# Sketched attention and a ReLU expert layer: token order taken at the PSUM reads, and other edits

## The chip, the cores and the metric

The kernel runs on one core of a Trainium2 chip. The metric is device time in microseconds. Engines are named as the profile names them: PE is TensorE (matmuls; its weight loads are PEld), DVE is VectorE, ACT is ScalarE, POOL is GpSimd, SP issues most of the transfers. Every engine works through its instructions in the order in which the program gives them.

## What is computed

For each of 4 batches and 4 heads (1088 tokens, 32 features) keys and queries go through two small matrices S1 and S2 (8 x 32), and the feature of a token is the product of all pairs. Attention without softmax follows, and then a layer on all 4352 tokens:

```python
def phi(x):
    a = np.einsum('rd,bhsd->bhsr', S1, x)
    b = np.einsum('rd,bhsd->bhsr', S2, x)
    return np.einsum('bhsi,bhsj->bhsij', a, b).reshape(*x.shape[:-1], r * r)
q_p, k_p = (phi(q), phi(k))
kv = np.einsum('bhsf,bhsd->bhfd', k_p, v)
z = np.sum(k_p, axis=2)
num = np.einsum('bhsf,bhfd->bhsd', q_p, kv)
den = np.einsum('bhsf,bhf->bhs', q_p, z)[..., None] + 1e-06
x = num / den                       # (4352, 128) after heads are put side by side
h = x @ w_in                        # 128 -> 2048
g = np.maximum(h, 0.0) + alpha * np.minimum(h, 0.0)
return g @ w_out                    # 2048 -> 128
```

## The kernel before

Every piece of work is an `op` with an engine (or several), a planned duration, what it depends on, and the buffers it uses. `plan` places the ops one after the other by those planned numbers and thereby fixes the order of instructions on each engine and the buffer that each gets; the chip then runs that fixed order. An op that may run on ACT or DVE goes to the one where the plan has it end sooner.

PSUM has eight banks. Bank 7 collects the output of the expert layer. The other seven are shared: `ph` gives banks to the expert layer's first matmuls (four at most), `pa` all banks of the attention (six at most).

**Keys** (`keys`, `kfeat`), per batch and pair of heads: DVE turns the keys block by block (`turn`, L482, tile kT); PE forms both small features (L450); an evacuation puts them in tile ab (L216 on ACT or L218 on DVE); POOL, or DVE for the first half of batch 0, multiplies all pairs (L463, tile kp); PE then forms kv (L500, L508, with L514 and L517 for the last 64 tokens). Small steps on DVE, ACT and PE (zm L528 to L531, fin L537 and L538, zz L547 and L548) make the weights kvW and zc.

**Queries** (`queries`, `q_main`), per batch: DVE turns all 1024 columns (L557, tile qT). PE forms the first feature, round *a*, in eight array tiles of 32 x 64 with 512 columns each (L564, `rnd`). Two ACT copies bring round a to SBUF (L216, tile aq, 128 x 1024 each). Round *b* forms the second feature, in two ops of four tiles each. Two DVE multiplications (L577) read b from PSUM and multiply it into aq. Then PE forms den and num (L592), DVE turns the denominators (L601, called dT), takes reciprocals (L607, L608), spreads them (L610) and multiplies (L615, tile xT, bf16). Batch 0 does the part from den on in two halves. The moving operand of rounds a and b is read in the order h, t, j, so neighbouring columns are 32 elements apart in qT.

**Expert layer** (`mlp`), 8 chunks of 512 tokens and one of 256: 16 times a matmul with w_in (L675), a relu on ACT (L681) or DVE (L683) into tile rh, and a matmul with w_a (L693), then one with W (L689); DVE turns the result (L699) and SP stores it. As alpha * min(h, 0) = alpha * h - alpha * max(h, 0), w_a is w_out times (1 - alpha), and W is w_in times alpha * w_out; both are computed at the start from the loaded weights (L385 and L394, POOL and ACT; L410, L421).

**Start.** SP issues the loads in the order of the program: k0 in two halves, v0 in four pieces of 256-byte rows, the rests, w_in, w_out, then k, q and v of batches 1 to 3. ACT issues the small rows and q0. Until the expert layer begins, matmuls on a zero tile (L332, warming matmuls) fill PE's order, their number set by the plan's gaps.

Of the kernel before, what the change touches and what calls it, by code (L numbers as in the profile page):

```python
# [48 lines left out]
OWN = 80  # L49
AHEAD = {"pe": 120, "act": 150, "dve": 250, "pool": 300, "sp": 0}  # L50


def plan(ops, classes):
# [39 lines left out]
    while waiting:  # L93
        shut, can = set(), []
        for o in waiting:
# [8 lines left out]
            fits = []  # L104
            for e in o.eng:
                t = max([at, free_at[e]] + [d.end + SEM if d.on != e else d.free if e == "pe" else d.end + OWN for d in o.deps])
                fits.append((t + o.dur[e], t, e))
            end, t, e = min(fits)
# [31 lines left out]
def kernel(  # L140
# [40 lines left out]
    def pa(n=1):  # L181

        return Buf("ps", n, "pa", PA_MOST, [6, 0, 1, 2, 3, 4, 5] if n == 1 else [0, 2, 4])
# [10 lines left out]
    def sb(b):  # L194
        return tiles[b.cls][b.slot]

    PA_MOST, PH_MOST = 6, 4
# [31 lines left out]
    state = {"t": 2800.0}  # L229
    loads = {}  # L230

    def load(name, eng, dst, src, nbytes, rate=290.0):
        if nbytes < 1 << 14:
            t = 3500.0
# [42 lines left out]
    def load_v(b):  # L277
        for t in range(4):
# [10 lines left out]
    load_main("q", q_sb, q, 0, "act")  # L289
    load_v(0)  # L290
    load_rest("k", k_rs[0], k, 0)
    load_rest("v", v_rs[0], v, 0)
    load("w_in", "sp", w_in_f, moe_w_in, 1 << 20)
    load("w_out", "sp", w_out_f, bass.AP(tensor=moe_w_out.tensor, offset=moe_w_out.offset,
                                         ap=[[DM, 128], [DM * 128, NC], [1, DM]]), 1 << 20)
    for b in range(1, B):
        load_k(b)
# [177 lines left out]
    def keys(b, due, kp_eng):  # L475
        halves = []
        for hp in range(2):
# [44 lines left out]
        bs, bz, bf = Buf("fs"), Buf("fs"), pa()  # L522
# [260 lines left out]
```

## Time and profile before

| | |
|---|---|
| median of 3 runs | 142.74 us (140.89 to 142.9) |
| the profiled execution | 143.26 us, of which the span of the trace is 141.3 us |
| busy in the span | PE 92%, DVE 65%, ACT 52%, POOL 16% |
| mean granted clock of PE | 0.953 of full |
| first and last matmul of the expert layer | 23.9 us and 133.9 us |

Times in the rows below are microseconds from the start of the span, or durations. [...] A matmul of f32 data shows as two instructions, since it takes two passes. In the chain that ended last each row lasts until the next link begins, so successive matmuls show their true spacing there, while the groups give the duration of single instructions, which overlap.

### The profile page before, as it was taken

What the parts mean: (1) busy time and instruction counts of PE and PEld (TensorE: products, weight loads), DVE (VectorE), ACT (ScalarE), POOL (GpSimd) and SP (SyncE); (2) the same over time, 40 slices, a digit from 0 to 9 for tenths busy, and PEclk for the clock granted to TensorE, in tenths of its full rate; (3) what the DMA queues carried; (4) which work ended last, traced back from release to release, by engine and by line L of the source; (5) the groups of instructions that cost most, each with busy time, mean ns of one, the idle gap of its engine ahead of it and who ended that gap; (6) DMA issues with size and microseconds to landing.
All of it is one profiled execution on the core that took longest, in us unless ns stands there. A gap on an engine that the chain in (4) does not pass through costs nothing.

```text
span 141.3 us, 3073 instructions
## 1 busy us (share of the span) xinstructions
PE 130.2 (92%) x1222; PEld 55.9 (40%) x1237; DVE 92.3 (65%) x168; ACT 72.8 (52%) x139; POOL 22.4 (16%) x20
## 2 busy tenths in 40 slices
PE   6999998999998999999999999999999999999910
PEld 2376142667212337543143364440423444445500
DVE  3661469999996797585468954174658957777500
ACT  3020466992644577637136676280437686666610
POOL 2005068790000000900000009000000000000000
PEclk9999999999999999999959999997579999999995
DMA  3989993899600400400004004000040040130400
GB/s 120 285 148 369 312 274 57 248 262 321 102 14 0 77 0 0 74 5 0 5 0 74 0 1 73 5 0 0 5 74 0 0 74 0 27 56 2 75 12 25
DMA packets 33906, 11.22 MB, mean 79 GB/s; under 512 B 28884, under 2 KB 33252, under 8 KB 33764
## 3 DMA queue, kind: packets, MB, share of 16 engines
q1 hardware_dynamic: 33252, 10.49, 31.6%
q10 hardware_dynamic: 640, 0.54, 1.2%
q8 instruction: 9, 0.15, 0.5%
q14 instruction: 5, 0.04, 0.1%
HBM read 8.80 MB, written 2.23 MB: 78 GB/s over the span
## 4 chain that ended last, share of the span: by engine, by line
PE 88%; DVE 2%; POOL 2%; issue 2%; ACT 2%; ACTq 0%; DVEq 0%
PE ps L675 23%; PE ps L693 23%; PE ps L564 15%; PE ps L592 7%; PE ps L332 6%; PE ps L450 5%; PE ps L500 3%; PE ps L689 2%; POOL kp__71 L463 2%; PE ps L421 1%; PE ps L514 1%; PE ps L410 1%; PE ps L538 1%; DVE dt__78 L601 1%; DVE rr__80 L610 1%
## 5 line engine op out<-in xcount | busy, mean ns | idle before, releaser
L681 ACT ACTIVATE rh__82<-ps 128x512 bf16<-128x512 f32 (+1 forms) x36 | 21.3, 592 | 16.5 <-PE ps L675 14.2
L675 PE MATMUL ps<-xT__94,w_in_bf 128*128 128x512 bf16 (+1 forms) x77 | 27.0, 369 | 1.9 <-DVE xT__94 L615 0.6
L675 PEld LDWEIGHTS <-w_in_bf 128*128 128x128 bf16 x144 | 14.3, 101 | 26.1 <-issue 15.6
L693 PEld LDWEIGHTS <-w_a_bf 128*128 128x128 bf16 x144 | 14.2, 102 | 26.2 <-issue 14.2
L675 PE MATMUL ps<-xT__95,w_in_bf 128*128 128x512 bf16 x62 | 23.3, 383 | 0.5 <-issue 0.4
L681 ACT ACTIVATE rh__83<-ps 128x512 bf16<-128x512 f32 (+1 forms) x26 | 14.7, 564 | 12.4 <-PE ps L675 11.2
L564 PE MATMUL ps<-qT__74,Sab 32*64 32x512 f32 x96 | 17.8, 1044 | 0.0
L693 PE MATMUL ps<-rh__82,w_a_bf 128*128 128x512 bf16 (+1 forms) x44 | 16.7, 380 | 0.1
L683 DVE TENSOR_SCALAR rh__84<-ps 128x512 bf16<-128x512 f32 (+1 forms) x17 | 10.6, 625 | 7.6 <-PE ps L675 7.3
L681 ACT ACTIVATE rh__84<-ps 128x512 bf16<-128x512 f32 x22 | 13.1, 596 | 4.3 <-PE ps L675 4.2
L683 DVE TENSOR_SCALAR rh__83<-ps 128x512 bf16<-128x512 f32 x16 | 11.0, 691 | 6.2 <-PE ps L675 6.2
L693 PE MATMUL ps<-rh__83,w_a_bf 128*128 128x512 bf16 (+1 forms) x38 | 14.2, 374 | 0.1
L463 POOL TENSOR_TENSOR kp__70<-ab__67 128x1024 f32<-128x1024 f32 x3 | 5.9, 1954 | 49.6 <-ACT ab__67 L216 49.6
L693 PE MATMUL ps<-rh__84,w_a_bf 128*128 128x512 bf16 (+1 forms) x36 | 13.7, 380 | 0.0
L216 ACT COPY aq__76<-ps 128x1024 f32<-128x1024 f32 (+1 forms) x8 | 6.7, 850 | 11.1 <-PE ps L564 11.1
L332 PE MATMUL ps<-zero 128*128 128x512 bf16 x38 | 11.1, 439 | 1.3 <-DVE tab L324 1.2
L577 DVE TENSOR_TENSOR aq__76<-ps,aq__76 128x1024 f32<-128x1024 f32 (+1 forms) x8 | 8.2, 1022 | 5.3 <-PE ps L564 5.3
L463 POOL TENSOR_TENSOR kp__71<-ab__68 128x1024 f32<-128x1024 f32 x4 | 8.1, 2033 | 8.9 <-ACT ab__68 L216 8.7
L681 ACT ACTIVATE rh__85<-ps 128x512 bf16<-128x512 f32 (+1 forms) x11 | 5.7, 521 | 2.9 <-PE ps L675 2.8
L683 DVE TENSOR_SCALAR rh__82<-ps 128x512 bf16<-128x512 f32 (+1 forms) x10 | 6.1, 612 | 1.7 <-PE ps L675 1.5
L699 DVE STREAM_TRANSPOSE oT__91<-ps 128x512 f32<-128x512 f32 x8 | 5.7, 716 | 2.2 <-PE ps L689 1.8
L332 PEld LDWEIGHTS <-zero 128*128 128x128 bf16 x39 | 4.0, 112 | 7.3 <-issue 3.6
(113 smaller groups left out, 169.5 us busy)
## 6 DMA issues: line engine op xcount, KB each, us to landing
out_dram<-oT__91 SPq DMA_DIRECT2D x34, 64.0 KB, 1.9
v<-in_v_dram SPq DMA_DIRECT2D x16, 128.0 KB, 5.5
k<-in_k_dram SPq DMA_DIRECT2D x3, 512.0 KB
q<-in_q_dram SPq DMA_DIRECT2D x3, 512.0 KB, 7.0
w_in_f<-in_moe_w_in_dram SPq DMA_DIRECT2D x1, 1024.0 KB, 5.0
k<-in_k_dram SPq DMA_DIRECT2D x2, 256.0 KB, 2.9
q<-in_q_dram ACTq DMA_DIRECT2D x1, 512.0 KB, 6.0
kr<-in_k_dram SPq DMA_DIRECT2D x4, 32.0 KB, 3.4
```

The costliest lines, as they stand in the source:

```text
L216: nc.scalar.copy(dst, src)
L332: nc.tensor.matmul(PS[:, 7], zero[:, :128], zero, start=True, stop=True, skip_group_check=True)
L450: nc.tensor.matmul(ps(bf)[:, j * 64:(j + 1) * 64], sb(bT)[:, j * 128:(j + 1) * 128], S12blk.rearrange("p h c -> p (h c)"), start=True, sto ...
L463: (nc.vector if e == "dve" else nc.gpsimd).tensor_tensor(out=dst, in0=i0, in1=i1, op=ALU.mult)
L564: nc.tensor.matmul(dst, bview(Sab[32 * t:32 * t + 32, i], [[1, R]]), moving(sb(bq), t, c), start=True, stop=True)
L577: mu.append(op("dve", dv(2 * nf), lambda e, x=x: nc.vector.tensor_mul(sb(aq)[:, 2 * x:2 * x + 2, :nf], ps(b2[x])[:, :, :nf], sb(aq)[:, 2 * ...
L592: nc.tensor.matmul(dst, w, mv, start=True, stop=True, skip_group_check=True)
L675: nc.tensor.matmul(ps(b)[:, :n], w_in_bf[:, c * 128:(c + 1) * 128], xs(), start=True, stop=True)
L681: nc.scalar.activation(sb(br)[:, :n], ps(b)[:, :n], ACTF.Relu)
L683: nc.vector.tensor_scalar_max(sb(br)[:, :n], ps(b)[:, :n], 0.0)
L693: nc.tensor.matmul(ps(bo)[:, :n], w_a_bf[:, c], sb(hs[c][1])[:, :n], start=c == 0, stop=False)
L699: o = op("dve", dv(n), lambda e: nc.vector.transpose(bview(sb(boT), [[1, n]]), ps(bo)[:, :n]), [last], [bo, boT], 80, t0 + TG * n / 512, f ...
```

## The change

- `moving` for the main queries reads qT in the order h, j, t: runs of 16 neighbouring elements. The columns of a and b therefore stand in PSUM in the order h, j, t, and the two ACT copies (`told`, `line`) and the two DVE multiplications read PSUM with a step of 16 elements and write aq in the order that den and num read as before.
- Round b is one op of eight tiles; it takes four banks at once.
- The stream `pa` is split: `pk` for keys (three banks at most), `pq` for queries (six at most).
- Batch 0's keys are turned by PE (transpositions against the identity, L451 in the new numbering) with an ACT copy out of PSUM each, and DVE's turn is left out there. v0 is loaded as one transfer to suit.
- q0 is issued by SP, behind k0; k1 is issued ahead of w_in and w_out.
- In `plan`, DVE's duration counts 1.2 times where an op may choose its engine. Sixteen of the 144 relus move from DVE to ACT (48 and 96 before, 32 and 112 now). 22 warming matmuls stand in PE's order, and 39 before.

```diff
+BIAS = {"dve": 1.2}
...
-                fits.append((t + o.dur[e], t, e))
-            end, t, e = min(fits)
+                fits.append((t + o.dur[e] * BIAS.get(e, 1), t, e))
+            _, t, e = min(fits)
+            end = t + o.dur[e]
...
-    def pa(n=1):
-        return Buf("ps", n, "pa", PA_MOST, [6, 0, 1, 2, 3, 4, 5] if n == 1 else [0, 2, 4])
+    def pk():
+        return Buf("ps", 1, "pk", PK_MOST, [6, 5, 4, 3, 2, 1, 0])
+
+    def pq():
+        return Buf("ps", 2, "pq", PQ_MOST, [0, 2, 4])
...
-    PA_MOST, PH_MOST = 6, 4
+    PK_MOST, PQ_MOST, PH_MOST = 3, 6, 4
+    KPE = [True, False, False, False]
...
     def load_v(b):
+        if KPE[b]:
+            load_main("v", v_sb, v, b)
+            return
...
     load_k(0, parts=2)
-    load_main("q", q_sb, q, 0, "act")
+    load_main("q", q_sb, q, 0)
     load_v(0)
     load_rest("k", k_rs[0], k, 0)
     load_rest("v", v_rs[0], v, 0)
+    load_k(1)
     load("w_in", "sp", w_in_f, moe_w_in, 1 << 20)
...
-            o = kfeat(None, need, due + 10 * hp,
+            srcs = [k_sb[b][:, 2 * hp + h, 4 * x:4 * x + 4].rearrange("p j d -> p (j d)")
+                    for x in range(2) for h in range(2)] if pe else None
+            o = kfeat(srcs, need, due + 10 * hp,
...
+        def told(a):
+            return a.rearrange("p b (h j t) -> p (b h) t j", h=H, j=NJ) if nf == 512 else a
+
+        def line(a):
+            return a.rearrange("p b (h t j) -> p (b h) t j", h=H, j=NJ) if nf == 512 else a
...
-                e, sb(aq)[:, 2 * x:2 * x + 2, :nf], ps(b1[x])[:, :, :nf]), [o], [b1[x], aq], LA, due + 2 + x, tag + "ac"))
-        bo_ = []
-        for x in range(2):
-            bo_.append(op("pe", nf * (1.7 if x else 0.2) + 20, rnd(1, b2, x), [o], [bq, b2[x]], 200 if x else 200 + nf * 1.5, due + 4 + x / 2, tag + "b"))
+                e, line(sb(aq)[:, 2 * x:2 * x + 2, :nf]), told(ps(b1[x])[:, :, :nf])), [o], [b1[x], aq], LA, due + 2 + x, tag + "ac"))
+        o = op("pe", nf * 1.7 + 40, rnd(1, b2), [o], [bq] + b2, 200, name=tag + "b")
...
-            mu.append(op("dve", dv(2 * nf), lambda e, x=x: nc.vector.tensor_mul(
-                sb(aq)[:, 2 * x:2 * x + 2, :nf], ps(b2[x])[:, :, :nf], sb(aq)[:, 2 * x:2 * x + 2, :nf]),
-                [bo_[x], ac[x]], [b2[x], aq], 80, due + 5 + x, tag + "mul"))
+            def mul(e, x=x):
+                a = line(sb(aq)[:, 2 * x:2 * x + 2, :nf])
+                nc.vector.tensor_mul(a, told(ps(b2[x])[:, :, :nf]), a)
+            mu.append(op("dve", dv(2 * nf), mul, [o, ac[x]], [b2[x], aq], 80, name=tag + "mul"))
...
-            return qT[32 * t:32 * t + 32, :, :, 16 * c:16 * c + 16].rearrange("p h j t -> p h t j")
+            return qT[32 * t:32 * t + 32, :, :, 16 * c:16 * c + 16]
```

PE, round b of batch 2, before (x4 counts the tiles of a half; L693 and L675 are expert matmuls):

```order
L675 MATMUL ps<-xT__95,w_in_bf 128x512
L564 MATMUL ps<-qT__75,Sab 64x512 x4
L693 LDWEIGHTS w_a_bf
L693 MATMUL ps<-rh__82,w_a_bf 128x512
L675 LDWEIGHTS w_in_bf
L675 MATMUL ps<-xT__95,w_in_bf 128x512
L564 MATMUL ps<-qT__75,Sab 64x512 x4
```

The same place now (L584 is the rounds' line, L712 and L694 the expert matmuls):

```order
L694 MATMUL ps<-xT__95,w_in_bf 128x512
L712 LDWEIGHTS w_a_bf
L712 MATMUL ps<-rh__83,w_a_bf 128x512
L584 MATMUL ps<-qT__75,Sab 64x512 x8
L694 LDWEIGHTS w_in_bf
L694 MATMUL ps<-xT__95,w_in_bf 128x512
```

Both halves have become one entry with eight tiles.

PE at the start, now, from the last of the nine leading warming matmuls (L451 transposes keys, L361 the rows, L460 forms the key features, L342 is a warming matmul):

```order
L342 MATMUL ps<-zero 128x512
L451 MATMUL ps<-ident,k_101 128x128 x4
L361 MATMUL ps<-ident,rows 128x32
L451 MATMUL ps<-ident,k_101 128x128 x4
L460 MATMUL ps<-S12blk,kT__64 128x64 x4
L460 MATMUL ps<-S12blk,kT__65 128x64 x4
L342 LDWEIGHTS zero
L342 MATMUL ps<-zero 128x512
L342 LDWEIGHTS zero
L342 MATMUL ps<-zero 128x512
L584 MATMUL ps<-qT__74,Sab 64x512 x8
L451 MATMUL ps<-ident,kr_113 128x128
```

Before, twelve warming matmuls stood between the rows' transposition and the key features, and round a of batch 0 came behind kv; now it comes ahead of it.

DVE ahead of the first expert matmul, before (L547 and L548 are zz, L601 is dT, k_102 are batch 1's keys):

```order
L547 TENSOR_TENSOR fs__97<-ps,M_124 128x32
L548 TENSOR_REDUCE zc_144<-fs__97 128x4
L218 CAST w_in_bf<-w_in_f 128x512 x2
L601 STREAM_TRANSPOSE dt__78<-ps 128x512
L607 TENSOR_SCALAR dt__78<-dt__78 128x16
L608 RECIPROCAL dt__78<-dt__78 128x16
L610 STREAM_TRANSPOSE rr__80<-dt__78 128x512
L615 TENSOR_TENSOR xT__94<-ps,rr__80 128x2x2x128
L482 STREAM_TRANSPOSE kT__64<-k_102 128x2x4x32 x2
L482 STREAM_TRANSPOSE kT__65<-k_102 128x2x4x32 x2
L577 TENSOR_TENSOR aq__76<-ps,aq__76 128x1024
```

And now (L493 turns keys, L560 and L561 are zz, L597 is the multiplication, L620 is dT):

```order
L493 STREAM_TRANSPOSE kT__64<-k_102 128x2x4x32 x2
L560 TENSOR_TENSOR fs__97<-ps,M_124 128x32
L561 TENSOR_REDUCE zc_144<-fs__97 128x4
L223 CAST w_in_bf<-w_in_f 128x512
L597 TENSOR_TENSOR aq__76<-ps,aq__76 128x1024
L620 STREAM_TRANSPOSE dt__78<-ps 128x512
L626 TENSOR_SCALAR dt__78<-dt__78 128x16
L627 RECIPROCAL dt__78<-dt__78 128x16
L629 STREAM_TRANSPOSE rr__80<-dt__78 128x512
L634 TENSOR_TENSOR xT__94<-ps,rr__80 128x2x2x128
```

Batch 1's keys and the second multiplication of batch 0 have moved ahead of dT.

## Rows read from the trace of the kernel before

**Rows 1.** The page: PE's busy share, and its granted clock in 40 slices.

```profile
PE 130.2 (92%) x1222; PEld 55.9 (40%) x1237; DVE 92.3 (65%) x168; ACT 72.8 (52%) x139; POOL 22.4 (16%) x20
PEclk9999999999999999999959999997579999999995
```

**Rows 2.** The page: the chain that ended last, shares by line.

```profile
PE ps L675 23%; PE ps L693 23%; PE ps L564 15%; PE ps L592 7%; PE ps L332 6%; PE ps L450 5%; PE ps L500 3%; PE ps L689 2%; POOL kp__71 L463 2%; PE ps L421 1%; PE ps L514 1%; PE ps L410 1%; PE ps L538 1%; DVE dt__78 L601 1%; DVE rr__80 L610 1%
```

**Rows 3.** The chain in order of time: start, us, what. Batches 1 and 2.

```profile
42.00 1.86 PE ps L564 x8
...
62.24 1.89 PE ps L564 x16
...
66.35 1.86 PE ps L564 x8
...
68.75 1.86 PE ps L564 x8
...
71.58 0.43 PE ps L675
...
74.16 1.02 PE ps L592 x16
...
75.71 0.22 PE ps L675
```

**Rows 4.** Stretches: us, then busy (count) by engine, PEclk, DMA share, GB/s.

```profile
39.40:41.26 1.86, 1.86 (x9) 0.20 (x10) 1.86 (x3) 0.61 (x2) 0.00 (x0) 1.00 0.04 9
97.09:98.96 1.87, 1.87 (x10) 0.21 (x10) 0.95 (x1) 0.00 (x0) 0.00 (x0) 0.60 0.00 0
46.42:47.44 1.02, 1.02 (x18) 0.18 (x18) 0.69 (x1) 0.83 (x2) 0.00 (x0) 1.00 0.38 70
103.01:104.65 1.64, 1.64 (x17) 0.23 (x18) 0.69 (x1) 0.34 (x1) 0.00 (x0) 0.61 0.58 99
```

**Rows 5.** Stretches of the busy part and the dips: PE, PEld, DVE, ACT, POOL, PEclk.

```profile
24.00:136.00 112.00, 108.49 (x1001) 46.38 (x1013) 79.54 (x135) 64.99 (x122) 14.73 (x9) 0.95 0.24 50
24.00:42.00 18.00, 17.79 (x247) 9.18 (x252) 17.72 (x30) 11.93 (x22) 7.01 (x5) 1.00 0.79 188
70.20:73.50 3.30, 3.14 (x12) 1.44 (x10) 1.72 (x4) 0.75 (x2) 0.00 (x0) 0.50 0.00 0
97.40:104.30 6.90, 6.68 (x34) 1.82 (x27) 3.66 (x6) 2.33 (x5) 0.00 (x0) 0.51 0.12 21
```

**Rows 6.** Groups by line and shape: count, then busy us, mean ns of one.

```profile
L681 ACT ACTIVATE rh__82<-ps 128x512 bf16<-128x512 f32 x35 | 20.9, 598 | 15.5 <-PE ps L675 13.1 <-PE ps L689 2.1
...
L577 DVE TENSOR_TENSOR aq__76<-ps,aq__76 128x1024 f32<-128x1024 f32 x6 | 7.4, 1226 | 5.3 <-PE ps L564 5.3
L216 ACT COPY aq__76<-ps 128x1024 f32<-128x1024 f32 x6 | 6.0, 1011 | 11.1 <-PE ps L564 11.1
...
L482 DVE STREAM_TRANSPOSE kT__65<-k 128x256 f32<-128x256 f32 x8 | 4.5, 643 | 0.0
...
L557 DVE STREAM_TRANSPOSE qT__75<-qr 128x256 f32<-128x256 f32 x1 | 0.4, 436 | 0.0
```

**Rows 7.** DVE in order of time at the start: start, us, instructions, idle before.

```profile
3.62 1.09 DVE L482 STREAM_TRANSPOSE kT__64<-k 128x256 f32<-128x256 f32 x2 [1.38 <-DMA k<-in_k_dram]
...
8.26 1.25 DVE L557 STREAM_TRANSPOSE qT__74<-q 128x1024 f32<-128x1024 f32 x1 [2.34 <-DMA q<-in_q_dram]
```

**Rows 8.** The chain in order of time: the start.

```profile
5.43 2.70 PE ps L332 x12
8.13 1.75 PE ps L450 x16
...
10.35 2.28 POOL kp__71 L463
...
12.67 1.01 PE ps L500 x57
...
23.89 0.38 PE ps L675
```

More of the change, by code (lines that the diff above doesn't have):

```diff
@@ L226, in at @@
         return T0 + g * TG
-    state = {"t": 2800.0}
+    state = {"t": 2600.0}
     loads = {}
@@ L233, in load @@
         if nbytes < 1 << 14:
-            t = 3500.0
+            t = 3700.0
         else:
@@ L296 @@
     for b in range(1, B):
-        load_k(b)
+        if b > 1:
+            load_k(b)
         load_main("q", q_sb, q, b)
@@ L434, in kfeat @@
         n = len(srcs) if turn is None else 4
-        bT, bf = Buf("kT"), pa()
+        bT, bf = Buf("kT"), pk()
         if turn is None:
-            bt = pa()
+            bt = pk()
             def tr(e):
@@ L476, in keys @@
         halves = []
+        pe = KPE[b]
         for hp in range(2):
@@ L485, in keys @@
             need = got(f"k{b}") if f"k{b}" in loads else got(f"k{b}.{hp}")
-            o = kfeat(None, need, due + 10 * hp,
+            srcs = [k_sb[b][:, 2 * hp + h, 4 * x:4 * x + 4].rearrange("p j d -> p (j d)")
+                    for x in range(2) for h in range(2)] if pe else None
+            o = kfeat(srcs, need, due + 10 * hp,
                       lambda bab=bab: bview(sb(bab), [[1, 256]]),
-                      lambda bkp=bkp: bview(sb(bkp), [[1, 1024]]), [bab], [bkp], kp_eng[hp], f"k{b}.{hp}", turn)
+                      lambda bkp=bkp: bview(sb(bkp), [[1, 1024]]), [bab], [bkp], kp_eng[hp], f"k{b}.{hp}", None if pe else turn)
             halves.append((o, bab, bkp))
         m, i = divmod(b, 2)
-        bk = pa()
+        bk = pk()
         def kv(e):
@@ L499, in kv @@
                 for h in range(H):
-                    nc.tensor.matmul(ps(bk)[32 * h:32 * h + 32, :R], v_sb[b][:, h, 2 * t + x],
+                    nc.tensor.matmul(ps(bk)[32 * h:32 * h + 32, :R], v_sb[b][:, h, 4 * x + t if pe else 2 * t + x],
                                      bview(kp[h // 2], [[1, 1024]])[:, ((2 * x + h % 2) * 4 + t) * R:][:, :R],
@@ L521, in keys @@
         o = op("pe", 200, kvr, [o, rest_k[m]] + got(f"vr{m}"), [bk], 200, name=f"kvr{b}")
-        bs, bz, bf = Buf("fs"), Buf("fs"), pa()
+        bs, bz, bf = Buf("fs"), Buf("fs"), pk()
         zt = lambda: bview(sb(bz), [[1, 32]])
@@ L553, in queries @@
     def queries(tag, needs, due, qsrc, nf, moving, bs, nums, ncol, xmul, bx, parts=1):
-        bq, b1, b2, aq = Buf("qT"), [pa(2), pa(2)], [pa(2), pa(2)], Buf("aq")
+        bq, b1, b2, aq = Buf("qT"), [pq(), pq()], [pq(), pq()], Buf("aq")
         n = qsrc.shape[1] if len(qsrc.shape) == 2 else None
         o = op("dve", dv(n), lambda e: nc.vector.transpose(bview(sb(bq), [[1, n]]), qsrc), needs, [bq], 80, due, tag + "T")
+        def told(a):
+            return a.rearrange("p b (h j t) -> p (b h) t j", h=H, j=NJ) if nf == 512 else a
+        def line(a):
+            return a.rearrange("p b (h t j) -> p (b h) t j", h=H, j=NJ) if nf == 512 else a
         def rnd(i, bufs, x=None):
@@ L582, in queries @@
         for part in range(parts):
-            bd, bn, dt, rr = pa(2), pa(2), Buf("dt"), Buf("rr")
+            bd, bn, dt, rr = pq(), pq(), Buf("dt"), Buf("rr")
             ncp = ncol // parts
```

## The prediction

> **What bounds the kernel now.** I read the busy shares first. TensorE (PE) is busy for 92% of the span, and the line of granted clocks under the slices falls in two places in mid span (a 5, and 7 5 7) [rows 1]. The chain that ended last says the same: 23 + 23% of the span are the two matmuls of the expert layer (L675, L693), 15% is one attention line, L564, and no other engine holds more than 2% [rows 2]. So what TensorE issues is what the kernel takes, and its most expensive attention line is worth taking apart.
>
> In order of time, one batch pays L564 three times: round a (eight tiles, 16 instructions since f32 takes two passes) 1.89 us, then the two halves of round b, four tiles each, 1.86 us each [rows 3]. Half the tiles cost the same time, so the time belongs to the streaming of 512 columns, not to the tiles. L592, also eight f32 tiles over 512 columns, takes 1.02 us [rows 3]. What differs is how the moving operand is read: L592 reads runs of 128 neighbouring elements; L564 reads `p h t j`, one element every 32. A second view settles whether that is the cause: a half round at the full clock took 1.86 us, one at 0.60 of it also about 1.87, while L592 went from 1.02 to 1.64 us at 0.61 [rows 4]. L592 follows TensorE's clock; L564 doesn't, so it waits for its operand.
>
> [...]
>
> [...] From 24 to 136 us PE idles 3.5 us of 112. [...]
>
> **The change, part by part.** *Token order moved to the evacuations.* `moving` now reads runs of 16 neighbouring elements, and ACT's copy and DVE's multiplication read PSUM at a step of 16 elements. A round then costs between 1.02 (L592's reads) and 1.89 us (nothing gained). I take 1.03: the runs are far nearer to L592's than to single elements. *Round b in one.* Two halves become one round of eight tiles. Together a batch falls from 1.89 + 1.86 + 1.86 = 5.61 to 2 x 1.03 = 2.06 us, 3.55 saved. Batches 1 to 3 lie on PE's busy stretch: 3 x 3.55 = **10.65 us**. Batch 0 belongs to the start, below.
>
> *The price on the other side*: 8 copies on ACT, now 1.01 us each, and 8 multiplications on DVE, 1.23 us each [rows 6], read PSUM with a step. The trace of before has no such read. The nearest row is a DVE transposition that writes SBUF at a step of four elements (L482), 643 ns for 256 elements, where the same size unstepped takes 436 (L557): 0.2 us per 256, so 0.8 us per 1024. Below, nothing: the copy takes 1011 ns and the multiplication 1226 for 1024 elements, about one a nanosecond, and if the element count alone sets that, a step changes nothing. A gain is excluded, since the count is the same. I take nothing, being nearer to the same instructions than to a transposition, and keep 0.8 us per instruction for the range.
>
> [...]
>
> *The clock.* Within the dips 3.3 + 6.9 = 10.2 us run at half; about 2.0 of these are slow rounds, which don't follow the clock. The other 8.2 would take 4.1 us less. Batch 1 has the same rounds, its last one from 42.00 us on [rows 3], and no dip there [rows 1], so it is close; with 2.06 us of denser rounds in place of 5.61 I take the dips as gone: **-4.1**, with 0 as the other end.
>
> *The start.* Before, nine warming matmuls and the rows' transposition end by 5.43 us, and twelve more run to 8.13, though batch 0's keys have been landing since 3.62 [rows 7]; the features begin at 8.13 [rows 8]. After, four transpositions of keys, the rows', and four more stand behind the nine. At 0.11 us an f32 instruction (1.75 us / 16) the first four end near 5.7; ACT's copy (512 columns, 0.60 us by L681, [rows 6]) ends near 6.3, the features start near 6.5: 1.6 us sooner. From there features, copy, POOL's product and kv follow as before (12.67 - 8.13 = 4.5 us [rows 8]), so kv starts near 11.1 and not 12.67. DVE's two turns of 1.1 us are gone, ACT's two copies take their place where ACT idled. From kv to the first expert matmul there were 23.89 - 12.67 = 11.2 us. Off this come round a (1.89, now ahead of kv; q0 is second on SP's queue, and the transposition that waited for it until 8.26 [rows 7] has till about 10) and 0.8 of round b; onto it come the second multiplication, now ahead of dT on DVE (1.2), and the part of a turn of batch 1's keys that fin doesn't cover (0.4): 10.1. First expert matmul at 21.2: **-2.7**. Bounds: if k1 lands late, DVE waits for it with kpr, the multiplication and zm queued behind, and kv's tail and the chain wait for those, so 0.5; if the second multiplication hides, 4.
>
> *Work moved ahead*: batch 1's feature matmuls (2 x 0.87, the 1.75 of batch 0's) and a quarter of the den/num matmuls (0.3) now run before that point, in the place of warming matmuls (39 to 22): **-2.0**. w_in and w_out stand 0.5 MB later in SP's queue, behind k1; PE's order has five L675 (1.1 us) ahead of the first L693 that needs w_out's product, and v0 comes as one transfer instead of four. Taken at nothing; uncovered, up to 1.
>
> *Bank streams and DVE's factor 1.2.* Sixteen evacuations move from DVE to ACT. In 24 to 136 us DVE is busy for 79.5 and ACT for 65.0 of 112 [rows 5], 72 each if shared, against about 97 that PE will need (112 - 10.65 - 4.1): no bound. A batch can still hold six of seven banks and leave one to the expert layer. What is late next: the den round waits for two multiplications, 2.4 us, behind b; batch 3's order has only fin and eight expert matmuls of 0.22 us [rows 3] in between, 1.8 us and fin. I count 0.5 us a batch, and 0.8 of the 2.28 us that POOL takes for batch 1's product, which now stands ahead of w_a and so of the first L693s: **+2.3**, between 0 and 5.
>
> **The sum**, against the profiled execution's own 143.26 us (span 141.3 and 2.0 around it; 0.4% above the median of the runs, 142.74): 143.26 - 10.65 - 4.1 - 2.7 - 2.0 + 2.3 = 126.1 us.
>
> **Rivals.** *Stepped PSUM reads cost 0.8 us each.* Round b needs the banks of the first copy, between a and b PE has some 1.7 us of other work: little. The multiplications become 4.0 us behind b where 2.0 to 3.9 of work stand: about 1.7 a batch, and 1.6 in the start: 126.1 + 5.1 + 1.6 = 132.8. For it: L482 pays for its step, and the moving operand pays for one in SBUF. Against it: no row here shows an engine pay for a step in PSUM.
>
> *The clock dips stay*: 126.1 + 4.1 = 130.2. For it: their cause is only placed by time.
>
> *The rounds don't shrink* (the 32-row tile is the cause, not the step): each stays at 1.88, only one of three per batch goes, 5.6 and not 10.65, and the dips stay: 126.1 + 5.0 + 4.1 = 135.2. Against it: half as many tiles took no less, and the clock test.
>
> *Nothing to speak of*: DVE, busy in the first expert chunks for 17.7 of 18 us [rows 5], sets them. The gains of the start and of one batch go, and the stepped price comes on top: 132.8 + 2.7 + 3.5 = 139.0, 2.6% under the median; with 1 us more it is no change. Against it: PE has no gap there that DVE fills.
>
> *Slower*: the clock. If a batch that holds six banks leaves the expert layer's h-relu-o loop with one, PE's stretch breaks up and the clock falls for good. At half, L675 and L693 cost 0.43 us each and not 0.22 [rows 3]. Without any gain of clock the sum is 130.2; it takes 13 us more to stand level and 16 to be 2% slower, that is 16 us of expert matmuls (264 x 0.22 and the last chunk's, some 61 in all) that take twice as long, a quarter of them; with a third, 150. For it: the dips exist. Against it: batches hold six banks before, too, and PE idles 3%.
>
> **Chances.** Forecast 0.57, stepped reads 0.18, dips stay 0.12, rounds don't shrink 0.04, hardly any gain 0.05, slower 0.04. A measurement of this kernel can tell about 2% from no change. Faster by over 2%: 0.91; within: 0.05; slower: 0.04. The forecast's own range, from its terms, is 121 to 131; the range reaches from 120.5 to 134.0, to hold the stepped reads and the dips.
>
> **What would show it.** Rounds of L584 near 1.03 us, both at full and less at half clock (else the step wasn't the cause); copies and multiplications at 1.01 and 1.23 us; first L694 near 21; no 5 in the line of clocks in mid span; PE's chain still near 88% with waits on DVE after round b of batch 3. Copies near 2 us, or a PE that waits for aq, would make the sum wrong first.

## The result, and the profile after

The changed kernel takes 131.48 us (median of four runs, 131.15 to 132.43); the kernel before took 141.88 on the same chip. The ratio is 0.928, with a 95% interval of 0.918 to 0.938. The forecast was 126.1 us: the direction held, the time lies inside the stated range of 120.5 to 134.0 (and just outside the 121 to 131 that the forecast's own terms gave), but 5 us of the expected gain are missing. The profiled execution took 131.18 us, so all sums below run from 143.26 to 131.18.

The kernel before varies by itself, over all its runs from 139.9 us, at a mean granted clock of 0.98, to 145.5, at 0.94, while the variants of the changed kernel mostly spread by 1.5% or less (one run each of x7 and xc lay 2 to 4% above the others) and are compared with each other by their medians.

The page of the changed kernel: PE's busy share, its granted clock in 40 slices, and the chain that ended last by line (cf. [rows 1, 2]).

```profile
PE 112.9 (87%) x1212; PEld 54.3 (42%) x1228; DVE 83.6 (65%) x148; ACT 79.4 (61%) x157; POOL 22.7 (18%) x20
...
PEclk9999998599599999999999999999999999999975
...
PE 69%; DVE 17%; ACT 5%; issue 2%; POOL 2%; DVEq 0%; ACTq 0%
```

The two dips of mid span are gone. Two others stand early (8 5 from 19.4 us, 5 from 32.4), and DVE, with 17%, holds part of the chain that PE held alone before.

The rounds in the chain in order of time (start, us, what), batch 2 of the changed kernel, and the groups of the multiplications, the copies and the `w_hi` casts, with the mean ns of one (cf. [rows 3, 6]).

```profile
64.32 1.04 PE ps L584 x16
...
68.12 1.04 PE ps L584 x16
```

```profile
L597 DVE TENSOR_TENSOR aq__76<-ps,aq__76 128x1024 f32<-128x1024 f32 x6 | 7.2, 1220 | 3.0 <-PE ps L584 3.0
...
L221 ACT COPY aq__76<-ps 128x1024 f32<-128x1024 f32 x6 | 5.9, 1013 | 2.2 <-PE ps L584 2.2
...
L223 DVE CAST w_hl<-w_b_f 128x512 bf16<-128x512 f32 x4 | 4.2, 1072 | 0.0
```

Two rounds of 1.04 us stand where 1.89, 1.86 and 1.86 stood. The stepped PSUM reads are free: 1220 against 1226 ns for a multiplication, 1013 against 1011 for a copy. The last row is the surprise: four casts on DVE, 1072 ns on average, where the same tile shape as `w_in_bf` takes 0.42 us.

Stretches of the changed kernel: us, then PE, PEld, DVE, ACT, POOL busy (count), PEclk, DMA share, GB/s (cf. [rows 5]).

```profile
22.60:24.60 2.00, 1.95 (x5) 0.74 (x6) 2.00 (x4) 1.05 (x2) 2.00 (x3) 0.50 0.35 109
...
28.00:32.50 4.50, 1.04 (x4) 0.20 (x3) 4.50 (x6) 2.09 (x4) 2.04 (x2) 0.97 1.17 299
32.50:36.00 3.50, 3.50 (x98) 2.44 (x97) 3.40 (x8) 0.59 (x1) 0.00 (x0) 0.55 1.04 173
36.00:122.00 86.00, 84.37 (x854) 38.30 (x850) 56.31 (x99) 62.10 (x123) 7.77 (x4) 1.00 0.15 26
```

From 36 us on the kernel does what was forecast: PE busy 84.4 of 86 us at the full clock. The loss lies ahead of that: PE works 1.04 of 4.5 us while DVE is busy throughout, and right behind that the clock is at half. What DVE does there, and what POOL does beside it (start, us, instructions):

```profile
19.39 1.34 DVE L626 TENSOR_SCALAR dt__78<-dt__78 128x16 f32<-128x16 f32 x1
...
25.54 3.38 DVE L223 CAST w_hl<-w_b_f 128x512 bf16<-128x512 f32 x2
28.84 1.75 DVE L395 TENSOR_TENSOR w_hl<-w_b_f,w_hl 128x512 bf16<-128x512 f32 x1
```

```profile
18.73 1.95 POOL L473 TENSOR_TENSOR kp__70<-ab__67 128x1024 f32<-128x1024 f32 x1 [7.24 <-DVE aq__76 L597]
...
25.28 1.95 POOL L473 TENSOR_TENSOR kp__71<-ab__68 128x1024 f32<-128x1024 f32 x1
27.18 2.85 POOL L395 TENSOR_TENSOR w_a_bf<-w_out_f,w_b_f 128x512 bf16<-128x512 f32 x2
```

The addition of 128 x 16 elements (L626) ends at 20.73, as POOL's product ends at 20.68; beside no POOL work it takes 0.18. The two casts end at 27.5 and 28.9; POOL's product ends at 27.23 and its first `w_a` near 28.6. PE's longest waits (line, waited for, us in total, times, longest):

```profile
PE ps L712 <- DVE rh__84 L702: 3.5, 1, 3.5
PE ps L694 <- DVE xT__94 L634: 2.3, 2, 2.2
```

The relu `rh__84` stands in DVE's order behind those casts and the subtraction; PE waits 3.5 us for it.

### The profile page after: what moved, and what is told of

It is laid out like the page before. It is cut to its first block, busy times and chain, and to the rows that moved or that the text cites. A ratio compares the mean times of both kernels' runs of the same rounds, so it can differ in the third digit from the quotient of the medians.

```text
span 129.4 us, 3045 instructions
## 1 busy us (share of the span) xinstructions
PE 112.9 (87%) x1212; PEld 54.3 (42%) x1228; DVE 83.6 (65%) x148; ACT 79.4 (61%) x157; POOL 22.7 (18%) x20
## 4 chain that ended last, share of the span: by engine, by line
PE 69%; DVE 17%; ACT 5%; issue 2%; POOL 2%; DVEq 0%; ACTq 0%
PE ps L712 20%; PE ps L694 20%; PE ps L584 6%; PE ps L611 6%; PE ps L460 5%; PE ps L513 4%; DVE aq__76 L597 4%; DVE w_hl L223 3%; PE ps L342 3%; POOL kp__71 L473 2%; DVE w_hl L395 2%; ACT rh__83 L700 2%; PE ps L431 1%; ACT rh__82 L700 1%; PE ps L708 1%
## 5 line engine op out<-in xcount | busy, mean ns | idle before, releaser
L694 PE MATMUL ps<-xT__94,w_in_bf 128*128 128x512 bf16 (+1 forms) x78 | 27.4, 376 | 3.1 <-DVE xT__94 L634 2.3
L700 ACT ACTIVATE rh__82<-ps 128x512 bf16<-128x512 f32 (+1 forms) x37 | 21.3, 575 | 13.2 <-PE ps L694 12.7
L694 PEld LDWEIGHTS <-w_in_bf 128*128 128x128 bf16 x144 | 14.2, 100 | 22.8 <-issue 11.1
L694 PE MATMUL ps<-xT__95,w_in_bf 128*128 128x512 bf16 x62 | 23.2, 379 | 0.1
L700 ACT ACTIVATE rh__84<-ps 128x512 bf16<-128x512 f32 (+1 forms) x29 | 16.5, 570 | 8.1 <-PE ps L694 8.0
L712 PEld LDWEIGHTS <-w_a_bf 128*128 128x128 bf16 x144 | 14.3, 101 | 16.8 <-issue 4.5
L700 ACT ACTIVATE rh__83<-ps 128x512 bf16<-128x512 f32 (+1 forms) x32 | 18.2, 569 | 3.5 <-PE ps L694 1.9
L712 PE MATMUL ps<-rh__84,w_a_bf 128*128 128x512 bf16 (+1 forms) x37 | 13.8, 372 | 3.6 <-DVE rh__84 L702 3.5
L712 PE MATMUL ps<-rh__82,w_a_bf 128*128 128x512 bf16 (+1 forms) x38 | 14.2, 374 | 0.1
L712 PE MATMUL ps<-rh__83,w_a_bf 128*128 128x512 bf16 (+1 forms) x38 | 14.1, 370 | 0.1
L702 DVE TENSOR_SCALAR rh__84<-ps 128x512 bf16<-128x512 f32 x10 | 6.9, 690 | 6.9 <-PE ps L694 6.8
L597 DVE TENSOR_TENSOR aq__76<-ps,aq__76 128x1024 f32<-128x1024 f32 (+1 forms) x8 | 8.0, 1018 | 3.0 <-PE ps L584 3.0
L342 PE MATMUL ps<-zero 128*128 128x512 bf16 x19 | 6.8, 494 | 1.4 <-DVE tab L334 1.2
L700 ACT ACTIVATE rh__85<-ps 128x512 bf16<-128x512 f32 x10 | 6.0, 598 | 3.2 <-PE ps L694 3.1
L702 DVE TENSOR_SCALAR rh__83<-ps 128x512 bf16<-128x512 f32 x9 | 6.1, 681 | 2.3 <-PE ps L694 2.2
L584 PE MATMUL ps<-qT__74,Sab 32*64 32x512 f32 x96 | 6.8, 624 | 0.0
L513 PEld LDWEIGHTS ps<-kp__70,v 128*32 128x32 f32 x128 | 4.5, 124 | 5.4 <-issue 5.0
L620 DVE STREAM_TRANSPOSE dt__78<-ps 128x1024 f32<-128x1024 f32 (+2 forms) x6 | 5.6, 933 | 0.9 <-PE ps L611 0.9
```

The lines of the kernel that those rows point to most:

```text
L342: nc.tensor.matmul(PS[:, 7], zero[:, :128], zero, start=True, stop=True, skip_group_check=True)
L584: nc.tensor.matmul(dst, bview(Sab[32 * t:32 * t + 32, i], [[1, R]]), moving(sb(bq), t, c), start=True, stop=True)
L597: nc.vector.tensor_mul(a, told(ps(b2[x])[:, :, :nf]), a)
L694: nc.tensor.matmul(ps(b)[:, :n], w_in_bf[:, c * 128:(c + 1) * 128], xs(), start=True, stop=True)
L700: nc.scalar.activation(sb(br)[:, :n], ps(b)[:, :n], ACTF.Relu)
L702: nc.vector.tensor_scalar_max(sb(br)[:, :n], ps(b)[:, :n], 0.0)
```

## Experiments

**Theory:** DVE stands still while POOL works, in instructions that read SBUF alone; the change put the four `w_hi` casts on DVE beside POOL's products, and that is the missing 5 us. **Rivals:** one of the forecast's own terms was too large (rounds, clock, start), or DVE was simply overloaded in the first expert chunk. The first six kernels take the change apart, the last six take up the first chunk.

### The parts of the change

**x4_token_undone.** The moving operand read one element every 32 again, copies and multiplications back to plain reads; the order of all engines as in the changed kernel.

```diff
-            return a.rearrange("p b (h j t) -> p (b h) t j", h=H, j=NJ) if nf == 512 else a
+            return a.rearrange("p b (h t j) -> p (b h) t j", h=H, j=NJ) if nf == 512 else a
...
-            return qT[32 * t:32 * t + 32, :, :, 16 * c:16 * c + 16]
+            return qT[32 * t:32 * t + 32, :, :, 16 * c:16 * c + 16].rearrange("p h j t -> p h t j")
```

> The changed kernel with the token order undone alone: PE reads qT at a step of 32 elements again, ACT and DVE read PSUM in line; the order of all engines is the same to the row. Theory (the step of the moving operand is what costs): all eight rounds take 1.88 instead of 1.04 us, copies and multiplications stay at 1.01 and 1.22; 6 x 0.84 = 5.0 us in batches 1 to 3 and up to 1.7 in the start, total 136 to 138 us, and dips of the clock behind the slow rounds as before the change if these are their cause (then up to 140). Rival (rounds shrank because eight tiles run as one op): no change, 131.5 us.

Measured: 136.83 us (135.87 to 137.69), 5.35 more than the changed kernel. Rounds of eight tiles take 1.89 us again in the chain, against 1.04: six of them on the busy stretch are 5.1 us. That this comes so near to 5.35 is in part a balance: the first expert matmul comes 1.0 us later, at 23.7, and PE's wait for the relu is 1.6 us shorter. Copies (1015 ns) and multiplications (1220) don't change, so the step in their PSUM reads costs nothing. And no dip in mid span comes back: from 36 to 122 us the granted clock is 1.00 (a stretch, columns as above). Three slow rounds per batch came with dips, two don't.

```profile
36.00:122.00 86.00, 84.74 (x821) 35.20 (x818) 54.94 (x96) 58.39 (x110) 7.77 (x4) 1.00 0.13 23
```

**x5_before_token.** The kernel before, with token order alone; round b still in two halves.

```diff
-            return qT[32 * t:32 * t + 32, :, :, 16 * c:16 * c + 16].rearrange("p h j t -> p h t j")
+            return qT[32 * t:32 * t + 32, :, :, 16 * c:16 * c + 16]
...
-                sb(aq)[:, 2 * x:2 * x + 2, :nf], ps(b2[x])[:, :, :nf], sb(aq)[:, 2 * x:2 * x + 2, :nf]),
+                line(sb(aq)[:, 2 * x:2 * x + 2, :nf]), told(ps(b2[x])[:, :, :nf]), line(sb(aq)[:, 2 * x:2 * x + 2, :nf])),
...
```

> The kernel before with the token order alone: same order of all engines as before, b still in two halves. Theory: round a 1.04, each half of b about 1.0 us instead of 1.86 (the columns cost, not the tiles); 3 x 2.5 = 7.6 us in batches 1 to 3 and 0.85 in the start: 141.9 - 8.4 = 133.5 us, and if the slow rounds cause the dips of the clock these vanish, down to 130 us. Rival (the reads with a step in PSUM cost ACT and DVE what PE gains): copies and multiplications near 1.8 and 2.0 us, total 139 us or more. Rival on the clock: dips stay, 133 to 134 us.

Measured: 134.87 us (134.72 to 135.53), ratio to before 0.961 [0.951, 0.970]. The chain shows round a and the halves of batch 2:

```profile
62.57 1.04 PE ps L570 x16
...
65.84 1.02 PE ps L570 x8
...
67.39 1.02 PE ps L570 x8
```

A half takes as long as a whole round, as before, but 1.02 and not 1.86. Token order is the larger part of the gain. Its profiled execution took 134.83 us, 8.4 less than that of before, where nine rounds of batches 1 to 3 (9 x 0.84 = 7.6 us) and the dips (4.1) would give 11.7: PE waited 2.7 us ahead of the first expert matmul, and the clock was at 0.50 to 0.56 from 23 to 29 us. Two `w_in` casts on DVE took 1.65 us there, beside POOL, where two take 0.76 in x7.

**x6_before_one_round.** The kernel before, with round b in one op, the slow reads kept.

```diff
-        for x in range(2):
-            bo_.append(op("pe", nf * (1.7 if x else 0.2) + 20, rnd(1, b2, x), [o], [bq, b2[x]], ...
+        o = op("pe", nf * 1.7 + 40, rnd(1, b2), [o], [bq] + b2, 200, name=tag + "b")
...
```

> The kernel before with round b as one op of eight tiles alone (strided moving reads as before, shared banks). Theory (512 columns cost 1.86 us whatever the tiles): one slow round less in batches 1 to 3, 3 x 1.86 = 5.6 us, 142 - 5.6 = 136.5 us; the dips of the clock in mid span go with them if three slow rounds a batch cause them (134.5). With token order alone 134.9 was measured, so the two are not additive: together they save 3 x 3.55, apart 7.6 and 5.6. Rival (the four banks at once make the expert layer wait): 139 us or more.

Measured: 142.57 us (ten runs), ratio 1.012 [1.006, 1.018]: no gain, and my number was wrong. The rounds did go (two of 1.9 to 2.0 us per batch), and so did the dips: 1.00 from 36 to 122 us. But the plan came out differently at the start. DVE there:

```profile
10.14 1.90 DVE L360 COPY Sab<-S12T 128x64 f32<-128x64 f32 x1
...
18.17 2.85 DVE L218 CAST w_in_bf<-w_in_f 128x512 bf16<-128x512 f32 x3
```

A copy of 128 x 64 takes 1.90 us (0.18 for the same size in the next line), from 10.14 to 12.04, while POOL's product runs from 10.04 to 11.99; the three casts run beside POOL's `w_b` and `w_a` (17.95 to 20.4) and take 2.85 and not 1.2. The first expert matmul comes at 26.5 us (before: 23.9), and the next stretch runs at half clock:

```profile
26.50:35.50 9.00, 8.96 (x45) 5.33 (x45) 5.29 (x9) 4.22 (x8) 5.02 (x3) 0.51 1.12 302
```

Three rounds (5.6) and the dips (4.1) should give 9.7 us, and the profiled execution (145.09) is 1.8 longer than that of before, so 11.5 have to be found. 2.6 us later, some 4.4 lost at half clock and 1.2 more of standing between 36 and 122 (PE busy for 83.4 us, and 84.6 before) are 8.2; the rest stays open, and the execution lies 2.5 us above the median. By these rows the mechanism of the theory is not the change's own: a new plan can run into it.

**x7_old_start.** The changed kernel with the start of before: batch 0's keys turned on DVE, q0 issued by ACT, the loads in their old order.

```diff
-    KPE = [True, False, False, False]
+    KPE = [False, False, False, False]
...
-    load_main("q", q_sb, q, 0)
+    load_main("q", q_sb, q, 0, "act")
...
-    load_k(1)
...
```

> The changed kernel with the old start: batch 0's keys turned on DVE, v0 in four pieces, q0 issued by ACT, k1 behind w_out; all else as changed. Theory (the new start brought the first expert matmul 1.2 us forward, and what it gained stands still behind DVE's blocked casts): same to 1.5 us slower, 131.5 to 133 us; in this order two casts are on ACT. Rival (the new start is worth its own 2.7 us, or more): 134 us or more. Rival (it is what drove POOL's products and DVE's casts into each other): faster, 129.5 to 130.5 us.

Measured: 131.66 us (130.97 to 136.06), the same as the changed kernel. The first expert matmul comes at 21.9, even 0.7 earlier. kv does start later, at 12.56 against 11.55, as the forecast had it; but from there 9.4 us remain and not 11.1, since DVE turns batch 1's keys only behind xT there. PE's wait ahead of the first expert matmul is 3.0 us, and the clock is at half from 22 to 30. So the new start, as it stands, is worth nothing; but in this order two of the `w_hi` casts are on ACT, and the run compares two plans, not the start alone.

**x9_shared_banks.** The changed kernel with keys and queries on one stream of six banks.

```diff
-        return Buf("ps", 1, "pk", PK_MOST, [6, 5, 4, 3, 2, 1, 0])
+        return Buf("ps", 1, "pa", 6, [6, 0, 1, 2, 3, 4, 5])
...
-        return Buf("ps", 2, "pq", PQ_MOST, [0, 2, 4])
+        return Buf("ps", 2, "pa", 6, [0, 2, 4])
```

> The changed kernel with one shared bank stream for keys and queries (six at most) as before the change. Theory (PE is not held by banks): within 1.5 us of 131.5, by where the casts fall. Rival (own streams are what lets round a of batch 0 and batch 1's keys run ahead): 133 us or more, first expert matmul later than 23.5.

Measured: 135.65 us (134.85 to 136.79), 4.2 more: both marks of the rival came true. The first expert matmul comes at 25.4, and three casts beside POOL take 4.08 us:

```profile
28.54 4.08 DVE L223 CAST w_hl<-w_b_f 128x512 bf16<-128x512 f32 x3
```

How much of the 4.2 us the streams themselves are worth stays open: in the profiled execution (136.79 us) PE waited 0.64 us for a late load at 6.7 us, the key features behind it took 3.3 us and not 2.0, and from 38 to 41 us the clock was at half.

**x8_no_bias.** The changed kernel without DVE's factor 1.2.

```diff
-BIAS = {"dve": 1.2}
+BIAS = {}
```

> The changed kernel without DVE's factor 1.2 in the plan; two of the four w_hi casts then fall to ACT and two stay on DVE, and 16 relus go back to DVE. Theory (the casts on DVE cost 1.2 each, the factor itself nothing): half of the 3.2 us that all four on ACT gave, 129.9, between 129 and 131.5 as the plan shifts. Rival (the factor is worth something by itself, as DVE is less busy): 132 or more.

Measured: 127.25 us (126.74 to 127.30), 4.2 *less* than the changed kernel, better than either side expected. 12 relus go back to DVE (44 there, 32 with the factor), and of the four `w_hi` casts two go to ACT. The other two meet POOL only in part:

```profile
24.17 0.61 DVE L223 CAST w_hl<-w_b_f 128x512 bf16<-128x512 f32 x1
...
25.90 0.98 DVE L223 CAST w_hl<-w_b_f 128x512 bf16<-128x512 f32 x1
...
27.40 4.04 DVE L395 TENSOR_TENSOR w_hl<-w_b_f,w_hl 128x512 bf16<-128x512 f32 x4
```

PE's wait of 3.5 us is gone (its longest for a relu is 0.5), and the granted clock is 1.00 from 20 to 36 us. The factor was meant to unload DVE; with it the plan gave ACT twelve more relus, and put the casts on DVE, next to POOL.

### The first expert chunk

**x1_casts_act.** The changed kernel, same order, the four `w_hi` casts issued on ACT.

```diff
-        o.emit(o.on)
+        o.emit("act" if o.name == "w_hi" else o.on)
```

> The changed kernel in its own order, with one edit: the four casts w_hl<-w_b_f are issued on ACT at the same place of the order instead of on DVE. In the changed kernel two of them took 3.3 us on DVE while POOL multiplied, and PE stood still for 3.5 us behind the relu queued after them. Theory (DVE's cast waits for POOL's instruction): DVE loses 3 to 4 us of blocked time, ACT's casts take 0.6 us each, the wait of L712 for rh on DVE shrinks to under 1 us, total 131.5 - 2 to 3.3 = 128.2 to 129.5 us. The w_lo products have two SBUF inputs and may wait in their place, which would eat part of it. Rival (DVE is simply overloaded there, a cast costs 0.42 us): 4 x 0.35 = 1.4 us at most, 130.1 us or more.

Measured: 128.25 us (127.82 to 128.54), 3.2 less. A cast on ACT takes 612 ns beside the same POOL work. DVE reaches the subtractions `w_lo` sooner, and now two of these meet POOL:

```profile
L221 ACT CAST w_hl<-w_b_f 128x512 bf16<-128x512 f32 x4 | 2.3, 612 | 0.0
...
25.58 4.10 DVE L395 TENSOR_TENSOR w_hl<-w_b_f,w_hl 128x512 bf16<-128x512 f32 x2
```

They take 2.0 us on average, 0.68 elsewhere. Nothing urgent stands behind them: PE's longest wait for a relu is 0.5 us.

**x2_no_eps.** The changed kernel, same order, without the addition L626 (the 1e-6 in the denominators).

```diff
-                nc.vector.tensor_scalar_add(t, t, EPS)
```

> The changed kernel without the addition of 1e-6 to the denominators (that part of the computation is left out). In the changed kernel this addition, 16 elements, took 1.34 us in batch 0's first half, ending with POOL's product, and 0.18 us elsewhere. Theory (it waited for POOL, the next DVE instructions don't): first expert matmul at 21.3 instead of 22.65 us, total 131.5 - 1.0 to 1.4 = 130.1 to 130.5 us. Rival (DVE as a whole stands behind POOL there, and the reciprocal or the spreading transposition waits instead): first expert matmul unchanged, 131.3 us.

Measured: 131.30 us (131.12 to 131.76), no change. The first expert matmul came 1.3 us earlier, at 21.3, as theory had it; but the casts still ended only when POOL was through (two took 3.38 us and ended at 27.7, POOL's product at 27.4), and the gain became wait:

```profile
PE ps L711 <- DVE rh__84 L701: 4.7, 1, 4.7
```

**xc_lo_on_pool.** The plan is told that `w_hi` runs on ACT and `w_lo` on POOL only.

```diff
-        hi = op(("act", "dve"), {"act": 615, "dve": 350}, ...
-        c_lo.append(op(("dve", "pool"), big, ...
+        hi = op("act", 615, ...
+        c_lo.append(op("pool", big, ...
```

> The changed kernel with the four casts w_hl on ACT and the four products w_lo on POOL, the plan told so: DVE has no instruction left in the first expert chunk that reads two SBUF inputs or casts from SBUF while POOL works, but the one addition in batch 0. Theory (DVE is blocked by POOL, 4.0 us at w_lo even with the casts on ACT): the wait of PE behind the relu on DVE in 28 to 32 us is gone, but POOL now has 4.8 us more ahead of the last w_a, so L712 of the second half of chunk 0 waits for POOL until about 34 us: 126.5 to 128.5 us against 128.25 with the casts alone moved. Rival (nothing but the casts' place counts): 128.2 us. Rival (POOL becomes the bound of the first chunk): 129.5 us or more.

Measured: 130.31 us (130.18 to 133.26), worse than theory's number. DVE has neither casts nor subtractions, but POOL's row grows (four `w_lo`, 4.5 us), the second half's addition L626 takes 1.91 us beside POOL's product, and PE waits 2.2 us ahead of the first expert matmul and 1.7 later for a small DVE copy; for POOL it waits nowhere there. To move all of it onto POOL prolongs what DVE can meet.

**xe_short_pool.** The direct test: the changed kernel, same order, DVE's instructions untouched, POOL's products of batch 1 and its `w_a` cut to a quarter of their columns; the other three quarters are left out of the result.

```diff
-        c_wa.append(op("pool", big, tt(w_a_bf[:, s], w_out_f[:, s], w_b_f[:, s], ALU.subtract), [wb], name="w_a"))
+        q = slice(s.start, s.start + 1)
+        c_wa.append(op("pool", big, tt(w_a_bf[:, q], w_out_f[:, q], w_b_f[:, q], ALU.subtract), [wb], name="w_a"))
...
+            if tag in ("k1.0kp", "k1.1kp") or tag in ("k1.0", "k1.1"):
+                dst, i0 = dst[:, :m // 4], i0[:, :m // 4]
...
```

> Every engine keeps the changed kernel's order and DVE's instructions are untouched; only POOL is relieved while DVE casts: batch 1's two key products and the four w_a pieces each work on a quarter of their columns (the rest of w_a is zeroed at the start; this part of the result is left out). Theory (DVE stands while POOL works): the addition in batch 0's denominators falls from 1.34 to about 0.2 us, the first expert matmul comes at about 21.4 instead of 22.65, the two casts take about 0.45 each instead of 1.65, and the time is 131.5 - 1.2 - 3 = about 127, near the forecast of 126.1. Rival (the casts are slow by themselves, or something else than POOL ends the first chunk): casts stay at 1.65, time 130 to 131.5.

Measured: 125.88 us (125.72 to 127.15), 5.6 less. The same four casts on the same engine, and the four subtractions, as groups (count, then busy, mean ns):

```profile
L398 DVE TENSOR_TENSOR w_hl<-w_b_f,w_hl 128x512 bf16<-128x512 f32 x4 | 2.7, 686 | 0.0
...
L223 DVE CAST w_hl<-w_b_f 128x512 bf16<-128x512 f32 x4 | 1.6, 411 | 0.0
```

411 ns and not 1072, 686 and not 944. The granted clock is 1.00 from 20 to 36 us. One part of the expectation missed: the first addition still takes 1.00 us,

```profile
19.38 1.00 DVE L633 TENSOR_SCALAR dt__78<-dt__78 128x16 f32<-128x16 f32 x1
```

as POOL's `w_b`, left whole, runs from 19.31 to 20.35, and the first expert matmul comes at 22.3 and not 21.4. So the casts' own slowness and an overloaded DVE are out: POOL beside them is the cause. One rival is left for a part of the time, that POOL's own work simply ends sooner here. It is small: in the changed kernel PE waits for POOL once, 0.8 us at 11 us, and xd, with POOL's work whole, comes to 126.81, so about 1 us of the 5.6 is left for it.

**xd_casts_eps_act.** x1_casts_act, with the first addition of batch 0's denominators on ACT too.

```diff
...
+                if dt is first_dt[0]:
+                    nc.scalar.activation(t, t, ACTF.Copy, bias=EPS)
+                else:
+                    nc.vector.tensor_scalar_add(t, t, EPS)
...
-        o.emit(o.on)
+        o.emit("act" if o.name == "w_hi" else o.on)
```

> The changed kernel with the w_hi casts on ACT, as in the run that gave 128.25, and with the addition in the first half of batch 0's denominators on ACT too; same order of everything else. Theory: ACT isn't held up by POOL, so the addition takes 0.3 instead of 1.33 us with some 0.1 for the way to ACT and back; first expert matmul at about 22.2 instead of 23.1, time about 127.3. Rival: DVE's next instruction (the reciprocal) or w_lo, still beside POOL, takes over the wait, as with the addition left out alone: 128.3.

Measured: 126.81 us (126.59 to 127.28). The addition takes 0.23 us on ACT, the first expert matmul comes at 21.5, 1.1 earlier than in the changed kernel, and this time the gain reaches the end: no cast stands behind it on DVE.

**xf_all_three.** xd_casts_eps_act without the factor 1.2.

```diff
-BIAS = {"dve": 1.2}
+BIAS = {}
```

> The changed kernel without DVE's factor 1.2, with all four w_hi casts and the first addition of batch 0's denominators on ACT: the three remedies together. Theory (all three pay by one and the same thing, DVE out of POOL's way in the first chunk; the factor itself is worth nothing): they don't add, since little of the wait is left, and the time is 126.0 to 127, as for the kernel with the addition and the casts on ACT (126.8) and the one without the factor (127.25). Rival (the factor costs by itself, through the relus that it moves to ACT): 127.25 - 3.4 - 1 = 123 to 124.5. A third outcome, 128 or more, would mean that ACT becomes the first chunk's bound.

Measured: 127.25 us (126.16 to 127.57). The remedies don't add, as theory had it: the factor by itself is worth no more than the runs spread by, and nothing shows a gain of another kind than DVE out of POOL's way.

xd_casts_eps_act has the lowest median of the complete versions, 126.81 us, ratio to before 0.900 [0.893, 0.908], 4.7 us less than the changed kernel; x8 and xf, at 127.25, are level with it within their spread.

## Why the prediction was right in its direction and 5 us off

**Rounds: right.** 1.04 us and not 1.03, twice per batch; three times 5.61 - 2.08 is 10.6 of the 10.65 us. Undoing the token order costs 5.35 where the rows make 5.1. Of the signs that the forecast named, these, the copies and multiplications, and the clock in mid span came true; a first L694 near 21 (22.65) and a chain that is 88% PE (69%) did not.

**Stepped PSUM reads: right.** Taken at nothing, they cost nothing; the rival that priced them at 0.8 us is out. A copy by ACT took 1013 ns with the step and 1011 without, a multiplication by DVE 1220 and 1226.

**Clock: right for mid span, by a reason that is only half borne out.** The dips are gone, but in x4, x5 and x6 as well (a granted clock of 1.00 from 36 to 122 us in each), wherever a batch had either fewer or faster rounds. The denser rounds that I counted on weren't needed, as x4 and x6 have two slow rounds a batch; that the third slow round starts a dip fits all of them (in the kernel before the half clock sets in at 70.1 and 97.4 us, within the third rounds of batches 2 and 3, which begin at 68.75 and 97.09 [rows 3, 4]), but no run shows why. The 4.1 us were read from one execution, at a mean granted clock of 0.953; what the dips cost in others is not shown. What the forecast left out is that the clock could fall anew at the start.

**The start: 1.45 us too hopeful.** kv came at 11.55 and not 11.1, as POOL's product took 2.66 us beside DVE's and not 2.28. From kv to the first expert matmul it took 11.1 and not 10.1: the addition L626 met POOL's product and took 1.34 and not 0.18.

**The stalls: the step that failed.** "I count 0.5 us a batch, and 0.8 of the 2.28": +2.3 us. Of the batch waits almost nothing came (behind round b of batch 3 PE waits 0.2 us for zc), but the first chunk took a wait of 3.5 us, 1.6 at half clock from 32.5 to 36 (3.5 x 0.45) and 1.0 from 22.6 to 24.6: with the 0.2, 6.3 in all, where the sum had 2.3 and a bound of 5. The same comes out of the whole: from the start of the first matmul with `w_in` to the start of the last it took 98.4 us (22.65 to 121.06) where the sum had 108.9 (23.89 to 132.79) - 10.65 - 4.1 - 2.0 + 2.3 = 94.45, 4.0 too many. With the 1.45 of the start that is 5.4; the ends give 0.3 back. x1 took 95.2 for the same stretch, xe 93.3. That the time still lies inside the range is luck: the range was widened for stepped reads that cost and for dips that stay, and neither came.

Two readings went wrong. First, of the change's moved work I priced the 16 relus that leave DVE, and not the four casts that come to it from ACT, though the order of the instructions shows them. Second, I ruled DVE out as a bound by its sum over 112 us, while the row of the first 18 us had it busy for 17.72 [rows 5], and didn't look at what these 17.72 are made of. It is not the number of casts that was too much: in xe all four stay on DVE, at 0.41 us each, and the time is 125.88, the forecast's. It is their price.

The price itself is a matter of who runs beside whom. In the traces DVE's casts and copies from SBUF, the addition in SBUF and the subtraction of two SBUF operands wait until POOL's running instruction is through: over all runs here the addition of 128 x 16 took 0.40 to 1.91 us beside POOL and 0.18 apart from it. Relus and multiplications that read PSUM don't wait (0.68 us in the changed kernel and 1.22 in x6, both beside POOL, as elsewhere), nor does ACT (612 ns). The two casts of the changed kernel took 1.65 us on average, where one takes 0.41 apart from POOL, and two subtractions in x1 2.0, where one takes 0.68, each ending 0.3 to 0.6 us behind the end of a POOL instruction. By what means POOL holds DVE up is not shown. Not everything that reads SBUF alone stands still, as the theory had it: beside POOL's `w_b` and `w_a` the changed kernel's reciprocal and its spreading transposition take 0.26 and 0.71 us, as they do in the second half, at 34.2 and 34.5 us, apart from POOL.

```profile
20.76 0.26 DVE L627 RECIPROCAL dt__78<-dt__78 128x16 f32<-128x16 f32 x1
21.05 0.71 DVE L629 STREAM_TRANSPOSE rr__80<-dt__78 128x512 f32<-128x512 f32 x1
```

The forecast has no term for this, though the rows had POOL busy for 7 of the first chunk's 18 us [rows 5] and the trace of before had the price, too: its four subtractions `w_lo` took 962 ns on average, the first of them 1.32 us beside POOL, and 0.68 apart from it.

```profile
29.58 1.32 DVE L385 TENSOR_TENSOR w_hl<-w_b_f,w_hl 128x512 bf16<-128x512 f32 x1
```

**Rivals.** "Hardly any gain, DVE sets the first chunk" named the right place, for a wrong reason and at too high a price; "dips stay" (130.2) came near the time by dips in mid span that weren't there.

## What to carry to other kernels

When an instruction moves to VectorE, look up what GpSimd runs at that moment: a short cast, copy or addition in SBUF took up to ten times its time there (a cast 1.65 us and not 0.41, a copy in x6 1.90 and not 0.18, an addition in xc 1.91 and not 0.18), and a planner that prices an engine's work by itself will walk into this with every new plan (x6 and the factor 1.2 show it). Judge a bound in the stretch where the work lands, not by sums over the whole. An operand order that hurts TensorE's reads (1.86 to 1.89 us a round, and 1.04 without it) was mended here for nothing where the data is read from PSUM anyway (1013 and 1220 ns, and 1011 and 1226 before).

## What the runs showed of the hardware

**The clock behind a wait.** PE's longest wait ahead of the first expert matmul, and the granted clock from 23 to 26 us (a value between 0.50 and 1.00 is a mean over both; the changed kernel has 0.50 from 22 to 25 us and 1.00 from 26 to 32):

| kernel | wait, us | granted clock, 23 to 26 us |
|---|---|---|
| xd_casts_eps_act, x2_no_eps | 1.0, 0.8 | 1.00, 1.00 |
| x8_no_bias, xe_short_pool, xf_all_three | 1.8 each | 1.00 each |
| after, x1_casts_act, xc_lo_on_pool, x4_token_undone | 2.2 each | 0.60, 0.64, 0.63, 0.50 |
| x5_before_token, x7_old_start | 2.7, 3.0 | 0.56, 0.50 |

The wait's length alone doesn't settle it: in x9 one of 1.4 us ahead of a round at 36.3 was followed by 0.50 from 38 to 41, in xd one of 1.3 at 30.8 by 1.00.

In x6 the wait was 2.9 and the matmul came at 26.5; from there to 35.5 the clock was 0.51. In x2 the later wait of 4.7 us was followed by 0.50 from 32 to 36, in the changed kernel that of 3.5 by 0.55. So these waits cost themselves and then again what PE had to do at half clock (in x6 some 4.4 of the 9 us from 26.5 on); that 1.1 us less for the addition was worth 1.4 at the end (x1 to xd: 128.25 to 126.81) fits, as the half clock behind it went as well (0.64 from 23 to 26 us in x1, 1.00 in xd), though the start varies by itself (22.65 in the changed kernel and 23.06 in x1, in the same order). The dips of the kernel before, in the midst of a busy PE, are not of this kind, and their cause is shown only so far: fewer or faster rounds end them.

**Runs of 64 bytes were enough.** With runs of 16 f32 elements in the moving operand a round takes 1.04 us, as L592 with runs of 128 (1.02); single elements 128 bytes apart take 1.86 to 1.89.
